# Two transposing DMAs inside SBUF in place of four DMA trips through DRAM in a convolution beside a gated MLP

## The chip, the cores and the metric

The kernel runs on one core of one Trainium2 chip. The metric is device time in microseconds (us), the median over runs of the whole launch. Before the change it is 251.94 us, the median of two runs at 250.64 and 253.25. The profiled execution, from which all durations below come, took 251.85 us. Its span, from the first to the last recorded instruction, is 249.6 us.

## What is computed

The inputs have 2048 positions (S) and 640 channels (D). `A_q` is x, and `xn` is its layer norm over channels. Two branches read `xn` and are added to x:

```
k_shift = four-tap causal convolution of k along S, taps per channel
kv  = k_shift * v
y   = causal convolution of kv with ssm_k along S (by rfft of length 4096) + kv * ssm_D
out = x + xn * y + (sigmoid(xn @ w_gate) * (xn @ w_up)) @ w_down
```

The gated MLP has 1728 hidden columns. All tensors are bf16.

## The kernel before

**The MLP** is the bulk of the matrix work. Positions are cut into four passes of 512. A pass runs 13 gate and up pairs (lines 258 and 270, five matmuls of 512 columns each), a closing pair for the last 64 hidden columns (282), and eight down products (297, 14 matmuls of 320 columns each). ScalarE takes the sigmoid from PSUM (261), VectorE multiplies (276) and adds the down products into x (300). From the second pass on, `xnT` is made by `xn_turn` (233): two DMAs that transpose 128 x 1280 elements each, within SBUF.

**The convolution** goes by five chunks of 128 channels. Each chunk passes these steps:

- `load_k`, `load_v`, `kv_op` (330 to 339): 16 VectorE operations that make kv.
- `h_tr` (315): 16 TensorE transposes of the filter. The weights that they load step by 16 elements, 32 bytes.
- `st1` (357): eight steps of four matmuls; ScalarE copies each step's 128 x 1024 fp32 result from PSUM (360).
- the first turn: four writes `wr1` (366) and four reads `rd2` (375) through a DRAM tile, 512 KB each.
- `st2` (385): four groups of 16 matmuls on 32 x 32 tiles, each followed by two ScalarE copies (388).
- `prod` (397, 399): per group a VectorE shuffle and a product.
- `inv1` (415): for each pair of groups 64 matmuls on 32 x 32 tiles with 256 columns; two ScalarE copies (420) into `ao`.
- the second turn: two writes `wr2` (427) and two reads `rdb` (437) through DRAM, 512 KB each.
- `inv2` (447): four steps of eight matmuls with 128 columns; VectorE multiplies by `xn` (451) and adds into x (452). Then `store` (303) writes out.

**The order** of every engine is fixed when the program is built. A planner in the kernel keeps a free time for every engine, walks along the MLP's steps on TensorE, and puts a step of the convolution between them when its estimated inputs are ready. Engines then run their lists in that order, waiting on semaphores. SyncE (SP, its queue is SPq) issues nearly all DMAs, also in order: a DMA that waits holds up those behind it. The buffers that matter are `psC`, two PSUM tiles for `st1`, `st2` and `inv1`, and the SBUF tiles `kx`, `kvh`, `t`, `xz`, `ao`, `bi`.

Of the kernel before, what the change touches and what calls it, by code (L numbers as in the profile page):

```python
# [19 lines left out]
P = 128  # L20
# [3 lines left out]
NQ = 4  # L24
# [33 lines left out]
def kernel(  # L58
# [31 lines left out]
    dr = ctx.enter_context(tc.tile_pool(name="dr", bufs=1, space=bass.MemoryType.DRAM))  # L90
# [21 lines left out]
    kxs = [res.tile([P, NB + 3, P], BF16, name="kx%d" % i) for i in range(2)]  # L112
    for kx in kxs:
        nc.gpsimd.memset(kx[0:1, 0:3, :], 0.0)
# [37 lines left out]
    def load_k(c, lo, hi):  # L152
        sync.dma_start(kxs[c % 2][:, lo + 3:hi + 3, :], kr[:, lo:hi, c * P:(c + 1) * P])

    def load_halo(c):
        cs = slice(c * P, (c + 1) * P)
        sync.dma_start(kxs[c % 2][16:P, 0:3, :], kr[15:P - 1, NB - 3:NB, cs])
        sync.dma_start(kxs[c % 2][1:16, 0:3, :], kr[0:15, NB - 3:NB, cs])

    def load_v(c, lo, hi):  # L160
        d = cin[c]
        if lo == 0:
            d["kvh"] = cv.tile([P, NB, 2, P], BF16, name="kvh", bufs=2)
        sync.dma_start(d["kvh"][:, lo:hi, 0, :], vr[:, lo:hi, c * P:(c + 1) * P])  # L164
# [17 lines left out]
    def ln_stats(g, i):  # L182
        b = 4 * g + i
        d = lns[g]
        if i == 0:
            d["st"] = cv.tile([P, 4, 2, nc.vector.BN_STATS_DIM], F32, name="st", bufs=2)
            d["mv"] = cv.tile([P, 4, nc.vector.BN_AGGR_DIM], F32, name="mv", bufs=2)
            d["var"] = cv.tile([P, 4], F32, name="var", bufs=2)
            d["rstd"] = cv.tile([P, 4], F32, name="rstd", bufs=2)
            d["nmr"] = cv.tile([P, 4], F32, name="nmr", bufs=2)  # L190
        for s2 in range(2):
            nc.vector.bn_stats(d["st"][:, i, s2, :], x[:, b, s2 * 320:(s2 + 1) * 320])  # L192
        nc.vector.bn_aggr(d["mv"][:, i, :], d["st"][:, i, :, :])
# [124 lines left out]
    def kv_op(c, n):  # L318
# [5 lines left out]
        kx = kxs[c % 2]  # L324
# [21 lines left out]
    def st1(c, n):  # L346

        h, n4 = divmod(n, 4)
        d = chunks[c]
        if n == 0:  # L350
            d["d1"] = dr.tile([P, 2, NB, 2 * P], BF16, name="d1", bufs=2)
        if n % 2 == 0:
            d["t1"] = cv.tile([P, 8, 2, P], BF16, name="t1", bufs=2)
        ps = psC.tile([P, 4, 2 * P], F32, name="ps1", tag="c")
        for i in range(4):
            b = 4 * n4 + i
            nc.tensor.matmul(ps[:, i, :], lhsT=S1[:, b, h, :], rhs=cin[c]["kvh"][:, b, :, :],  # L357
                             start=True, stop=True)
        o = 4 * (n % 2)
        nc.scalar.copy(out=d["t1"][:, o:o + 4, :, :].rearrange("p b s c -> p b (s c)"), in_=ps[:, :, :])  # L360
        d[n // 2] = d["t1"]

    def wr1(c, k):
        h, part = divmod(k, 2)
        d = chunks[c]
        sync.dma_start(d["d1"][:, h, 8 * part:8 * part + 8, :], d[k].rearrange("p b s c -> p b (s c)"))
# [3 lines left out]
    def rd2(s):  # L370

        c, s4 = divmod(s, 4)
        t2 = cv.tile([P, 8, 2 * P], BF16, name="t2", bufs=2)
        src = chunks[c]["d1"].rearrange("(r q) h b e -> r (q h b) e", q=NQ)
        sync.dma_start(t2[:, :, :], src[8 * s4:8 * s4 + 8].rearrange("r p e -> p r e"))
        groups[s] = dict(t2=t2)

    def st2(s):

        d = groups[s]  # L380
        d["xz"] = cv.tile([P, 3, 8, P], BF16, name="xz", bufs=3)
        ps = [psC.tile([P, 2, 2, 2, P], F32, name="ps2", tag="c") for _ in range(2)]
        for g in range(4):
            for q in range(NQ):
                nc.tensor.matmul(ps[q // 2][quad(g), q % 2, :, :, :], lhsT=SM[quad(q), 0, :],  # L385
                                 rhs=d["t2"][quad(q), 2 * g:2 * g + 2, :], start=True, stop=True)
        for n in range(2):
            nc.scalar.copy(out=d["xz"][:, 0:2, 4 * n:4 * n + 4, :].rearrange("p s k c -> p k s c"),  # L388
                           in_=ps[n].rearrange("p q e s c -> p (q e) s c"))
# [3 lines left out]
    def prod(s, n):  # L393

        xz = groups[s]["xz"]
# [6 lines left out]
    def inv1(y):  # L402
# [3 lines left out]
        if y2 == 0:  # L406
            d["d2"] = dr.tile([32, P, P], BF16, name="d2", bufs=2)
        ao = kxs[1][:, 0:NB, :] if y >= 7 and y % 2 else cv.tile([P, 16, P], BF16, name="ao")[:, :, :]
        ps = [psC.tile([P, 2, 512], F32, name="psa", tag="c") for _ in range(2)]
        for o in range(2):  # L410
            xz = groups[2 * y + o]["xz"]
            for i in range(2):
                for q in range(NQ):
                    for g in range(4):
                        nc.tensor.matmul(ps[g // 2][quad(q), g % 2, 256 * o:256 * o + 256], lhsT=SM[quad(g), 1 + i, :],  # L415
                                         rhs=xz[quad(g), 1 + i, 2 * q:2 * q + 2, :],
                                         start=(i == 0), stop=(i == 1))
# [6 lines left out]
    def wr2(y):  # L424
        c, y2 = divmod(y, 2)
        d = chunks[c]
        sync.dma_start(d["d2"][16 * y2:16 * y2 + 16].rearrange("r p c -> p r c"), d["ao", y])

    def rdb(c, n):

        d = chunks[c]
        if c >= 3 and n == 1:
            bi = kxs[0][:, 0:NB, :].rearrange("p (h b) c -> p h b c", h=2)
        else:
            bi = cv.tile([P, 2, 8, P], BF16, name="bi")[:, :, :, :]
        src = d["d2"].rearrange("r (q h b) c -> (r q) h (b c)", q=NQ, h=2)
        sync.dma_start(bi.rearrange("p h b c -> p h (b c)"), src[:, :, 1024 * n:1024 * n + 1024])
        d["bi", n] = bi

    def inv2(c, m):  # L440

        cs = slice(c * P, (c + 1) * P)
        bi = chunks[c]["bi", m // 2]
        ps = psG.tile([P, 4, P], F32, name="psb", tag="g")
        for i in range(4):
            for h in range(2):
                nc.tensor.matmul(ps[:, i, :], lhsT=TB[:, h, 4 * m + i, :], rhs=bi[:, h, 4 * (m % 2) + i, :],  # L447
# [70 lines left out]
    def emit(step):  # L518
# [3 lines left out]
        for eng, dur, need, make in ops:  # L522
            at = when(need)
            if eng == "DMA":
                free["SP"] = max(free["SP"], at) + 0.45
                free["DMA"] = max(free["DMA"], free["SP"] + 1.4) + dur
                end = free["DMA"] + 1.2
            else:
# [21 lines left out]
    def s_st1(c, n):  # L550
        def ops():
            mk, nd = C()
            n4 = n % 4
            k = 4 * c + n // 2
            o = [("PE", 0.45, [nd, "S1", ("kv", c, n4 // 2), ("h", c, n4 // 2)], [("st1", c, n)]),
                 ("ACT", 0.92, [("st1", c, n), prior("d1", k - 2)], [mk, ("t1", c, n)])]
# [3 lines left out]
    def s_wr1(c, i):  # L560
        return s_load(wr1, (c, i), 1.35, [("t1", c, 2 * i + 1)], [("d1", 4 * c + i)])

    def s_rd2(s):
        return rd2, (s,), lambda: [("DMA", 1.8, [("d1", 4 * (s // 4) + i) for i in range(4)]
                                    + [prior("st2", s - 2)], [("t2", s)])]

    def s_st2(s):
        def ops():
# [3 lines left out]
                    ("ACT", 0.92, [("st2", s), prior("inv1", (s - 3) // 2) if s > 2 else None], [m0]),  # L572
# [6 lines left out]
    def aofree(y):  # L579
        if y < 7:  # L580
            return [prior("d2", y - 1)]
        return [("kvn", 3, 15)] if y == 7 else [("d2", y - 2)]

    def s_inv1(y):
        def ops():
            m0, n0 = C()
            m1, n1 = C(1)
            return [("PE", 0.75, [n0, n1, ("prod", 2 * y + 1)], [("inv1", y)]),
                    ("ACT", 0.92, [("inv1", y)] + aofree(y), [m0]),
# [3 lines left out]
    def s_rdb(c, n):  # L593
        if c < 3:
            back = ("inv2", c, 1) if n else prior("inv2", c - 1, 3)
        else:
            back = (("inv2", 2, 3), ("inv2", 3, 1), ("kvn", 4, 15), ("inv2", 3, 3))[2 * n + c - 3]
        return rdb, (c, n), lambda: [("DMA", 1.0, [("d2", 2 * c), ("d2", 2 * c + 1), back], [("bi", c, n)])]

    def s_inv2(c, m):  # L600
        def ops():
            mk, nd = G()
            return [("PE", 0.48, [nd, ("bi", c, m // 2), ("xn", m, 3) if m else None, "TB"], [("inv2", c, m)]),
                    ("DVE", 0.62, [("inv2", c, m)], [mk, ("yx", c, m)]),
                    ("DVE", 0.36, [("yx", c, m)], [("xa", c, m)])]
        return inv2, (c, m), ops

    def s_htr(c, part):
        def ops():
            mk, nd = G()  # L610
            return [("PE", 0.55, [nd, ("D", c), ("va", c)], [("htr", c, part)]),
                    ("ACT", 0.92, [("htr", c, part), prior("st1", c - 2, 7)], [mk, ("h", c, part)])]
# [13 lines left out]
    def s_load(fn, args, occ, need, make):  # L626
        return fn, args, lambda: [("DMA", occ, need, make)]

    chains = dict(sp=[], dve1=[], ln=[], kv=[], pool=[], act=[], inv=[], mid=[], front=[], out=[], sp_b=[], sp_k=[],
                  sp_v=[], sp_t=[], sp_h=[], bulk=[], sp_w1=[], sp_w2=[])  # L630
    for c in range(NC):
        if c:
            last = [prior("kvn", c - 2, 13)]
# [9 lines left out]
            for i in range(4):  # L643
                chains["sp_v"].append(s_load(load_v, (c, 4 * i, 4 * i + 4), 0.7, [prior("st1", c - 2, 7)],
# [6 lines left out]
        chains["sp_w1"] += [s_wr1(c, i) for i in range(4)]  # L651
        for s in range(4 * c, 4 * c + 4):
            chains["sp"].append(s_rd2(s))
            chains["mid"].append(s_st2(s))
            chains["dve1"] += [s_prod(s, 0), s_prod(s, 1)]
            if s % 2:
                chains["inv"].append(s_inv1(s // 2))
                chains["sp_w2"].append(s_load(wr2, (s // 2,), 2.4, [("ao", s // 2)], [("d2", s // 2)]))
        chains["sp_b"] += [s_rdb(c, n) for n in range(2)]
# [36 lines left out]
    def s_turn(g, i):  # L696
        return s_load(xn_turn, (g, i), 1.6, [("pass", g - 1), ("xn", g, i), ("xn", g, i + 1)], [("xT", g, i)])
# [53 lines left out]
    DUE = (8, 48, 52)  # L751
    slack = dict(bulk=3.0, sp_k=3.0, sp_v=3.0, sp_h=1.5, bulk2=1.5)

    def side(now, at):

        again = True
        while again:
            again = False
            for k in ("sp_x", "sp_w1", "sp", "sp_w2", "sp_b", "sp_t", "bulk", "sp_k", "sp_v", "sp_h", "bulk2", "out"):
# [21 lines left out]
    at, credit, TURN, TH = 0, 0, 6, 1.5  # L781
# [58 lines left out]
```

## Time and profile before

| what | value |
|---|---|
| profiled execution | 251.85 us, span 249.6 us |
| TensorE busy | 235.6 us, 94% of the span |
| VectorE busy | 185.1 us, 74% |
| ScalarE busy | 144.4 us, 58% |
| DMA queue q1 | 55.59 MB, 79.8% of 16 DMA engines' span |
| granted TensorE clock | 0.994 |

In the tables of groups a line names the source line, the engine, the operation and its tiles, then the count, the busy time in us and the mean ns of one instruction. PEld is TensorE's weight load, which runs beside its matmuls. The share of a page's chain of waits is the share of the span that the work that ended last spent on an engine. A timeline row has a start, a duration, and in brackets the idle time before it and what ended it. A matmul's duration in a row is longer than the distance to the next one, because matmuls are pipelined; where the path matters, distances between starts are used.

### The profile page before, as it was taken

The page shows a single profiled execution, that of the slowest core. Times are in us where ns is not written, and L with a number is a line of the kernel's source. Part 1 is how long each engine was busy: PE and PEld are TensorE (multiplying, and loading weights), DVE is VectorE, ACT ScalarE, POOL GpSimd, SP SyncE. Part 2 cuts the span into 40 slices and gives each one's busy share as a digit, 9 for nine tenths or more (in the row PEclk, how much of TensorE's full clock was granted, in tenths as well). Part 3 has the DMA queues.
Part 4 walks back from the last instruction along what each step waited for, and adds up shares of the span by engine and source line. Part 5 has one row for each costly group of instructions (what it writes and reads, how often), then busy time and mean ns, then how long its engine had stood idle before and what let it go on. Part 6 is the DMA issues. An engine that isn't in the chain of part 4 may idle for free.

```text
span 249.6 us, 5854 instructions
## 1 busy us (share of the span) xinstructions
PE 235.6 (94%) x2409; PEld 137.5 (55%) x2409; DVE 185.1 (74%) x346; ACT 144.4 (58%) x178; POOL 10.0 (4%) x24
## 2 busy tenths in 40 slices
PE   8799999998999999897999999999999999999970
PEld 2474555776445564565755456456765444466760
DVE  3627997529999999897789999789245865886253
ACT  2652366403888796445698778785665668663000
POOL 4300001000000020020000000000000000000000
PEclk9999999999999999999999999999999999999997
DMA  6998999999998999997589878398787454764544
GB/s 178 286 245 233 332 332 335 286 242 246 221 277 235 330 327 264 232 264 172 231 225 273 253 265 250 90 191 206 217 247 243 115 158 118 223 193 146 132 144 147
DMA packets 96294, 56.81 MB, mean 228 GB/s; under 512 B 56268, under 2 KB 89356, under 8 KB 96012
## 3 DMA queue, kind: packets, MB, share of 16 engines
q1 hardware_dynamic: 95692, 55.59, 79.8%
q10 hardware_dynamic: 576, 0.85, 1.1%
q8 instruction: 19, 0.31, 0.5%
q14 instruction: 7, 0.06, 0.1%
HBM read 36.12 MB, written 18.35 MB: 218 GB/s over the span
## 4 chain that ended last, share of the span: by engine, by line
PE 81%; DMA 7%; DVE 5%; SPq 4%; issue 1%; ACT 1%; DVEq 0%
PE pg L258 22%; PE pu L270 22%; PE pd L297 15%; PE ps L357 7%; DMA bi<-d 3%; PE psa L415 3%; PE psb L447 3%; PE ps L385 3%; DMA t<-d 2%; PE pg L248 2%; PE pg L282 2%; PE pht L315 2%; DMA x<-in_A_q_dram 1%; DVE st L192 1%; DVE yx L451 1%; SPq L164 1%
## 5 line engine op out<-in xcount | busy, mean ns | idle before, releaser
L297 PE MATMUL pd<-wd,hT 128*128 128x320 bf16 x448 | 64.2, 299 | 0.0
L258 PE MATMUL pg<-xnT,w 128*128 128x512 bf16 x250 | 62.2, 380 | 0.0
L270 PE MATMUL pu<-xnT,w 128*128 128x512 bf16 x250 | 62.2, 379 | 0.0
L297 PEld LDWEIGHTS <-hT 128*128 128x128 bf16 x448 | 43.2, 98 | 18.0 <-issue 1.4
L388 ACT CAST xz<-ps 128x1024 bf16<-128x1024 f32 x40 | 38.6, 1018 | 18.8 <-PE ps L385 18.8
L276 DVE TENSOR_TENSOR hT<-sig,pu 128x512 bf16<-128x512 bf16 x49 | 33.4, 681 | 17.2 <-PE pu L270 12.6
L261 ACT ACTIVATE sig<-pg 128x512 bf16<-128x512 f32 x52 | 31.5, 606 | 24.4 <-PE pg L258 21.7
L360 ACT CAST t<-ps 128x1024 bf16<-128x1024 f32 x40 | 38.8, 1016 | 8.7 <-PE ps L357 6.9
L270 PEld LDWEIGHTS <-w 128*128 128x128 bf16 x250 | 23.7, 98 | 27.0 <-issue 1.1
L258 PEld LDWEIGHTS <-w 128*128 128x128 bf16 x250 | 23.3, 98 | 26.7 <-issue 2.0
L300 DVE TENSOR_TENSOR x<-pd,x 128x320 bf16<-128x320 f32 x32 | 15.6, 490 | 24.7 <-PE pd L297 24.6
L399 DVE TENSOR_TENSOR xz<-xz 128x2048 bf16<-128x2048 bf16 x20 | 24.5, 1223 | 0.5
L357 PE MATMUL ps<-kvh,S1t 128*128 128x256 bf16 x160 | 21.6, 273 | 0.0
L336 DVE TENSOR_TENSOR acc<-acc,tmp 128x1024 bf16<-128x1024 bf16 x30 | 20.8, 692 | 1.0
L334 DVE TENSOR_TENSOR tmp<-kx,sc 128x1024 bf16<-128x1024 bf16 x30 | 20.5, 685 | 0.3
L420 ACT CAST ao<-psa 128x1024 bf16<-128x1024 f32 x16 | 15.4, 1015 | 6.7 <-PE psa L415 6.7
L357 PEld LDWEIGHTS <-S1t 128*128 128x128 bf16 x160 | 15.6, 98 | 5.8
L451 DVE TENSOR_TENSOR yx<-psb,xn 128x512 bf16<-128x512 f32 x20 | 13.8, 691 | 4.1 <-PE psb L447 2.8
L316 ACT COPY kvh<-pht 128x1024 bf16<-128x1024 bf16 x10 | 9.7, 1030 | 11.7 <-PE pht L315 11.7
L192 DVE BATCH_NORM_STATS2 st<-x 128x6 f32<-128x320 bf16 x32 | 13.8, 474 | 3.1 <-DMA x<-in_A_q_dram 3.1
L397 DVE STREAM_SHUFFLE xz<-xz 128x512 f32<-128x512 f32 x20 | 14.6, 728 | 0.0
L447 PEld LDWEIGHTS <-TBt 128*128 128x128 bf16 x160 | 9.4, 98 | 3.7 <-issue 1.9
(50 smaller groups left out, 139.9 us busy)
## 6 DMA issues: line engine op xcount, KB each, us to landing
d<-t SPq DMA_DIRECT2D x20, 512.0 KB, 4.2
t<-d SPq DMA_DIRECT2D x20, 512.0 KB, 5.4
d<-ao SPq DMA_DIRECT2D x8, 512.0 KB, 4.5
bi<-d SPq DMA_DIRECT2D x8, 512.0 KB, 5.0
hn<-in_A_ssm_k_dram SPq DMA_DIRECT2D x8, 256.0 KB, 4.5
kx<-in_A_k_dram SPq DMA_DIRECT2D x16, 128.0 KB, 4.8
kvh<-in_A_v_dram SPq DMA_DIRECT2D x16, 128.0 KB, 4.0
x<-in_A_q_dram SPq DMA_DIRECT2D x3, 640.0 KB, 6.2
```

Of the source, the lines that this page charges most:

```text
L258: nc.tensor.matmul(pg[:, :], lhsT=w[:, c, fc * P:(fc + 1) * P], rhs=xnT[:, :, c, :], start=(c == 0), stop=(c == NC - 1))
L261: nc.scalar.activation(sig[fc][:, :], pg[:, :], ACT.Sigmoid)
L270: nc.tensor.matmul(pu[:, :], lhsT=w[:, c, UP + fc * P:UP + (fc + 1) * P], rhs=xnT[:, :, c, :], start=(c == 0), stop=(c == NC - 1))
L276: nc.vector.tensor_tensor(hT[:, fc, :], sig[fc][:, :], pu[:, :], ALU.mult)
L297: nc.tensor.matmul(pd[:, :], lhsT=hT[:, fc, bb * P:(bb + 1) * P], rhs=wd[:, fc, es], start=(fc == 0), stop=(fc == NFC - 1))
L334: nc.vector.tensor_tensor(d["tmp"][:, :, :], kx[:, lo + 3 - m:hi + 3 - m, :], sb(m), ALU.mult)
L336: nc.vector.tensor_tensor(d["acc"][:, :, :], d["acc"][:, :, :], d["tmp"][:, :, :], ALU.add)
L357: nc.tensor.matmul(ps[:, i, :], lhsT=S1[:, b, h, :], rhs=cin[c]["kvh"][:, b, :, :], start=True, stop=True)
L360: nc.scalar.copy(out=d["t1"][:, o:o + 4, :, :].rearrange("p b s c -> p b (s c)"), in_=ps[:, :, :])
L388: nc.scalar.copy(out=d["xz"][:, 0:2, 4 * n:4 * n + 4, :].rearrange("p s k c -> p k s c"), in_=ps[n].rearrange("p q e s c -> p (q e) s c"))
L399: nc.vector.tensor_tensor(xz[:, 1:3, :, :], xz[:, 0:1, :, :].to_broadcast((P, 2, 8, P)), xz[:, 1:3, :, :], ALU.mult)
L447: nc.tensor.matmul(ps[:, i, :], lhsT=TB[:, h, 4 * m + i, :], rhs=bi[:, h, 4 * (m % 2) + i, :], start=(h == 0), stop=(h == 1))
```

## The change

The DRAM tiles and `wr1`, `rd2`, `wr2`, `rdb` go. In their place, `turn1` issues two transposing DMAs for each of the four groups of a chunk (128 x 1024 elements each), and `turn2` issues one for each of its two halves (128 x 2048). For that, ScalarE's copy after `st1` writes its result turned inside the partition: it reads PSUM with a step of 256 fp32 elements and writes runs of four bf16 with a step of 64 bytes. `inv2` reads its moving operand with a step of 32 elements, 64 bytes. Products of two groups share one tile, so `inv1` has half as many matmuls of twice the columns. There is one buffer in place of two or three for `kx`, `kvh`, the products and layer-norm statistics; `t1` now holds a whole chunk once, and `t2` has four buffers.

The planner is given new entries for the turns and new values for two of its constants, so that the order of all engines changes too. In the built program, the last `inv1` of the last chunk has no down product after it, where before it had 84 down matmuls; the last `st2` has 14 down matmuls between it and that `inv1`.

```
-    kxs = [res.tile([P, NB + 3, P], BF16, name="kx%d" % i) for i in range(2)]
+    kx = res.tile([P, NB + 3, P], BF16, name="kx")
...
-            d["kvh"] = cv.tile([P, NB, 2, P], BF16, name="kvh", bufs=2)
+            d["kvh"] = cv.tile([P, NB, 2, P], BF16, name="kvh")
...
-        nc.scalar.copy(out=d["t1"][:, o:o + 4, :, :].rearrange("p b s c -> p b (s c)"), in_=ps[:, :, :])
+            d["t1"] = cv.tile([P, 2 * P, 2, NB], BF16, name="t1")
+        nc.scalar.copy(out=d["t1"][:, :, h, 4 * n4:4 * n4 + 4], in_=ps.rearrange("p b e -> p e b"))
-    def wr1(c, k):
-        sync.dma_start(d["d1"][:, h, 8 * part:8 * part + 8, :], d[k].rearrange("p b s c -> p b (s c)"))
-    def rd2(s):
-        sync.dma_start(t2[:, :, :], src[8 * s4:8 * s4 + 8].rearrange("r p e -> p r e"))
+    def turn1(s):
+        c, s4 = divmod(s, 4)
+        t2 = cv.tile([P, 2, 8, P], BF16, name="t2", bufs=4)
+        for i in range(2):
+            e = P * i + 32 * s4
+            sync.dma_start_transpose(t2[:, i, :, :], chunks[c]["t1"][:, e:e + 32, :, :].rearrange("p e h b -> p (e h b)"))
...
-        d["xz"] = cv.tile([P, 3, 8, P], BF16, name="xz", bufs=3)
+            pairs[y] = cv.tile([P, 3, 2, 8, P], BF16, name="xz")
...
-                        nc.tensor.matmul(ps[g // 2][quad(q), g % 2, 256 * o:256 * o + 256], lhsT=SM[quad(g), 1 + i, :],
-                                         rhs=xz[quad(g), 1 + i, 2 * q:2 * q + 2, :],
+                    nc.tensor.matmul(ps[g // 2][quad(q), g % 2, :], lhsT=SM[quad(g), 1 + i, :],
+                                     rhs=pairs[y][quad(g), 1 + i, :, 2 * q:2 * q + 2, :],
...
-    def wr2(y):
-        sync.dma_start(d["d2"][16 * y2:16 * y2 + 16].rearrange("r p c -> p r c"), d["ao", y])
-    def rdb(c, n):
-        sync.dma_start(bi.rearrange("p h b c -> p h (b c)"), src[:, :, 1024 * n:1024 * n + 1024])
+    def turn2(y):
+            d["bi"] = cv.tile([P, P, 2, NB], BF16, name="bi")
+        sync.dma_start_transpose(d["bi"][:, 64 * y2:64 * y2 + 64, :, :].rearrange("p (g a) h b -> p g (a h b)", a=4),
+                                 d["ao", y].rearrange("p r c -> p (r c)"))
...
-                nc.tensor.matmul(ps[:, i, :], lhsT=TB[:, h, 4 * m + i, :], rhs=bi[:, h, 4 * (m % 2) + i, :],
+                nc.tensor.matmul(ps[:, i, :], lhsT=TB[:, h, 4 * m + i, :], rhs=bi[:, :, h, 4 * m + i],
...
-    DUE = (8, 48, 52)
+    DUE = (8, 56, 80)
...
-    at, credit, TURN, TH = 0, 0, 6, 1.5
+    at, credit, TURN, TH = 0, 0, 1, 1.5
```

## The prediction

> **What bounds the kernel now.** I read the page's busy table, slices and chain first.
>
> ```profile
> PE 235.6 (94%) x2409; PEld 137.5 (55%) x2409; DVE 185.1 (74%) x346; ACT 144.4 (58%) x178; POOL 10.0 (4%) x24
> ...
> PE   8799999998999999897999999999999999999970
> ...
> PE 81%; DMA 7%; DVE 5%; SPq 4%; issue 1%; ACT 1%; DVEq 0%
> ```
>
> TensorE is busy 235.6 of 249.6 us; the 14.0 us without it lie in the first slice and the last two. A step taken from another engine or a DMA wins nothing unless TensorE was waiting for it. So I read the table of waits for TensorE and its weight loads:
>
> ```profile
> PEld L385 <- DMA t<-d: 2.3, 2, 1.3
> ...
> PE ps L385 <- DMA t<-d: 1.7, 2, 0.9
> PE psb L447 <- DMA bi<-d: 1.6, 1, 1.6
> ```
>
> The columns are total us, times, longest. Weight loads and matmuls wait side by side, so the trips through DRAM cost TensorE 1.7 + 1.6 = 3.3 us: that is all the change can win in mid-stream. The rest is the tail, from the timeline:
>
> ```profile
> 225.41 0.73 DVE L397 STREAM_SHUFFLE xz<-xz 128x512 f32<-128x512 f32 x1
> ...
> 226.18 1.23 DVE L399 TENSOR_TENSOR xz<-xz 128x2048 bf16<-128x2048 bf16 x1
> ...
> 227.76 0.84 PE L415 MATMUL psa<-xz,SMt 32*32 32x256 bf16 x64
> ...
> 228.53 11.58 PE L297 MATMUL pd<-wd,hT 128*128 128x320 bf16 x84
> 228.62 1.93 ACT L420 CAST kx<-psa 128x1024 bf16<-128x1024 f32 x2 [3.97 <-PE psa L415]
> 230.57 0.37 SPq L427 DMA_DIRECT2D d<-kx  x1
> ...
> 239.95 1.06 PE L447 MATMUL psb<-bi,TBt 128*128 128x128 bf16 x16
> ```
>
> The last inv1 ends at 228.60. Its copies, write and read then run beside 84 down matmuls, and the first inv2 of the last chunk starts at 239.95, when these end. From there to the end of the span are 9.69 us: four VectorE steps of about 1.25 us (the products start at 240.60, 241.85, 243.11, 244.36), then the stores.
>
> **The tail after the change.** TensorE's work is the same but for two terms below. The new order has all 84 down matmuls ahead of the last inv1, so that step can start at 227.76 + (239.95 - 228.53 = 11.42) = 239.18, if the stream before it loses as much as now. What it waits for is later still. Only 14 down matmuls, 14 x (11.42 / 84 = 0.136) = 1.9 us, stand between the last st2 and it, while its input needs two copies (1.93, the pair at 228.62; st2's have the same shape), a shuffle (0.73), a product (1.23) and about 0.3 of handing over (0.02 to 0.2 at each hand in these rows): 4.2 us. TensorE waits 2.3.
>
> Behind inv1 nothing is left to hide anything. Two copies take it from 228.60 to 230.57 today, 1.97 us with the issue. Then comes the new turn. Its nearest row is the transposing DMA that the kernel has already, ten blocks of 128 x 128 within SBUF; one line's view has its time on SP's queue (least, median, most ns) and its landing from issue:
>
> ```profile
> L233 SPq DMA_TRANSPOSE xnT<-xn x6: 1342/1856/4044, 47.2 to 167.4; - x6
> ...
> DMA to landing us min/median/max: 3.5/4.4/6.2
> ```
>
> The last turn has 16 blocks, and the DMA engines are idle then. Bounds: 3.5 (ten blocks' least) and 6.2 x 1.6 = 9.9. I take the low side, 3.5 + 6 x 0.134 (1.342 / 10) = 4.3, with 0.4 for handing over: 4.7. Sum: 239.18 + 2.3 + 0.84 (inv1) + 1.97 + 4.7 + 9.69 = 258.7, against 249.64: **+9.0 us**.
>
> **TensorE's own terms.** inv2's moving operand now steps by 64 bytes. No matmul here streams with such a step; the nearest rows are weight loads, one with a step of 32 bytes and one without:
>
> ```profile
> L447 PEld LDWEIGHTS <-TBt 128*128 128x128 bf16 x160 | 9.4, 98 | 3.7 <-issue 1.9 <-DMA bi<-d 0.9
> ...
> L315 PEld LDWEIGHTS <-hn 128*128 128x128 bf16 x80 | 5.7, 148 | 0.1
> ```
>
> 128 stepped columns take 50 ns more. Weight loads hide beside matmuls, so sixteen h_tr steps take 1.00 us on the chain against 0.89 for sixteen inv2 matmuls: 7 ns more each. A moving operand has no such cover. Bounds: 0 and, no row excluding worse than the load's, twice 50 ns; I take 50. Four chunks of 32 matmuls: 128 x 50 = 6.4 us; in the last chunk only the first step's eight count (0.4), the others hide under VectorE's 1.25 us. **+6.8 us.**
>
> [...]
>
> inv1's 32 matmuls of 512 columns replace 64 of 256, the same columns. By st2 (16 of 512 in 0.44 us on the chain) they take 0.88, against 0.77 now; equal columns say no change. I take half of 0.11, ten times: **+0.5 us**.
>
> **What I cost at nothing.** *ScalarE's copy after st1* (40 of them, 1.016 us now) gets a stepped PSUM read; no row has one. Bounds: 1.0 and 2.0. The nearest is the taps' copy with an 8-byte step in SBUF (128x512, 0.664 us) beside the 128x512 sigmoid (0.606): 0.11 ns per element more, 1.13 us by that. ScalarE has 105 us free, and 4 us more over the kernel lie beside TensorE's work.
>
> *The first turn.* From the last st1 of a chunk to its first st2 the new order has 7 to 12 us of TensorE work. The need: a copy and its handing over (1.2), the first DMA on SP for eight blocks (1.1 to 1.8), the landing of the second (3.5 to 6.2): 5.8 to 9.2. The 3.3 us of waits today may go, or such waits replace them. I take neither.
>
> *SP and DMA traffic.* Fifty transposing DMAs cost SP between 0.134 and 0.228 us per block (1.342, and 13.65 us for the six over 60): 480 blocks, 64 to 109 us. The 60 removed issues were 0.33 to 0.53 each, 24 us. SP has room in sum. The 60 removed transfers were 31 MB of 56.8, the new turns are 15 MB read and written once.
>
> *Single buffers.* kvh's next v load waits for st1's last step, kx's for the chunk's last tap, the pair tile's copies for the inv1 before: all lie under 2 us or more of MLP work in the new order. VectorE's operations keep their count and sizes.
>
> **Sum.** 249.6 + 9.0 + 6.8 + 0.5 = 265.9 of span; the execution is 2.2 longer than its span (251.85 - 249.6), and 0.1 from the median shown. **268 us**, 6.4% slower.
>
> **Rivals.**
>
> *The step costs inv2 nothing*, or the 7 ns of h_tr: 268 - 6 = **262**. For it: the weight loads' excess is latency. Against: nothing hides a moving operand. 0.22.
>
> *The stepped PSUM read is slow*: ScalarE's copy at 2.0 us. st1's steps alternate two PSUM tiles, and a chunk's last five or six stand within 5 to 8 us of TensorE work. The last must wait for the copy of the second before it, four copies after the second step of the run: 4 us at 1.0, just covered, 8 at 2.0, so 3 to 4 us of TensorE lost in four chunks and about 1 in the spread-out last, 15 in all: **283**. Against: the taps' copy. 0.16.
> [...]
>
> *SP is held.* Chunk 1's v load stands on SP behind eight turn DMAs and two xn turns, and VectorE's list needs it about 20 us after them. At the median rate it lands about in time; at 4.0 us for ten blocks the eight take 25 us, and VectorE, hence the PSUM tiles of up, stands 4 to 12 us. Taken at 8: **276**. For: the six DMAs spread threefold. 0.12.
>
> *Not slower*: the trips through DRAM are what holds the present stream. Along the order, TensorE's distances add up to 5.3 us less than its clock shows from the first h_tr to the last down product, 3.3 of it the waits above. If short turns clear all of it, steps cost nothing and the last turn lands in 3.5, 249.6 - 5.3 + 8.2 + 2.2 = **255**, within 2%. To be faster, the tail too would have to be covered; the order leaves it only 1.9 us. 0.08.
>
> My forecast has 0.42. The range takes in the rivals from 257 (the second case, less 3.3 for waits that go and 1 for the landing) to 282. Left out are the last rival and half of the slow copies, 0.16. A measurement here tells about 2%, 5 us, from no change: faster (below 246.9) 0.03, within 0.08, slower (above 257.0) 0.89.
>
> **What would show it.** Behind the last down matmul, about 16 us of span with a last inv1, a DMA and then inv2; a last turn landing in 4 to 5 us; 16 inv2 matmuls in 1.6 to 1.8 us instead of 0.89; st1's copies near 1.1 us; TensorE's waits for turns in mid-stream no longer than 4 us. A first inv2 of the last chunk hidden under down products, or busy TensorE time falling, would prove me wrong.

## The result and the profile after

The changed kernel takes 282.27 us (median of 282.16 and 282.39) against 251.94: 1.120 times as long, 95% interval 1.095 to 1.145. The direction was right; the size was not. 268 was forecast, and 282.3 lies just beyond the end of the range at 282. The span of the profiled execution is 280.5 us, 30.9 more than before.

The page of the changed kernel: busy time by engine, the slices of TensorE and of its granted clock, and the chain.

```profile
PE 262.9 (94%) x2089; PEld 144.8 (52%) x2089; DVE 186.3 (66%) x346; ACT 144.3 (51%) x177; POOL 10.1 (4%) x23
...
PE   7899999999999999999999999999999999997072
...
PEclk9999999999999999999999999995999995999655
...
PE 3%; DMA 2%; issue 1%; DVE 0%; ACT 0%; ACTq 0%
```

VectorE and ScalarE have the busy time that they had (186.3 us against 185.1, 144.3 against 144.4). TensorE is busy 27.3 us longer, with 320 instructions fewer, so some of them became dearer. Two slices of the clock in mid-stream read 5, half speed. The same line of the kernel before has none:

```profile
PEclk9999999999999999999999999999999999999997
```

The chain could be followed back for 7% of the span only, which is no use here.

The groups by line and shape, of the changed kernel (count, then busy us and mean ns), name the dear ones:

```profile
L354 ACT CAST t<-ps 128x1024 bf16<-128x1024 f32 x40 | 39.1, 1016 | 11.4 <-PE ps L352 11.1
...
L429 PE MATMUL psb<-bi,TBt 128*128 128x128 bf16 x160 | 36.2, 393 | 6.4 <-DMA bi<-ao 6.4
...
L405 PE MATMUL psa<-xz,SMt 32*32 32x512 bf16 x320 | 6.5, 379 | 2.9 <-DVE xz L393 2.9
```

inv2's 160 matmuls are busy 36.2 us; before they were busy 8.6 + 2.1. ScalarE's copy with the stepped PSUM read is at 1016 ns exactly what the plain one was. The distance between inv2's matmuls is read from TensorE's timeline of the changed kernel, here at full clock in mid-stream:

```profile
82.60 3.62 PE L429 MATMUL psb<-bi,TBt 128*128 128x128 bf16 x16
86.05 1.05 PE L352 MATMUL ps<-kvh,S1t 128*128 128x256 bf16 x8
```

Sixteen take 86.05 - 82.60 = 3.45 us; the median distance from one to the next is 0.217. In the kernel before, sixteen start at 239.95 and the next sixteen here:

```profile
240.84 1.06 PE L447 MATMUL psb<-kx,TBt 128*128 128x128 bf16 x16
```

That is 0.89 us, 0.056 each. The moving operand with a step of 64 bytes costs TensorE four times the time, 0.161 us more per matmul.

The clock, in windows of the changed kernel around the second dip (us; busy time of TensorE and its weight loads, VectorE, ScalarE, GpSimd; granted clock; DMA share; GB/s):

```profile
234.00:235.00 1.00, 1.00 (x5) 0.49 (x4) 0.41 (x2) 0.00 (x0) 0.00 (x0) 0.50 0.97 181
...
238.00:239.00 1.00, 1.00 (x21) 0.28 (x19) 0.45 (x1) 0.10 (x1) 0.00 (x0) 1.00 1.04 307
```

and TensorE's timeline just there:

```profile
227.71 7.11 PE L429 MATMUL psb<-bi,TBt 128*128 128x128 bf16 x32
234.65 2.31 PE L256 MATMUL pg<-xnT,w 128*128 128x512 bf16 x5
236.75 1.69 PE L268 MATMUL pu<-xnT,w 128*128 128x512 bf16 x5
238.38 0.43 PE L378 MATMUL ps<-t,SMt 32*32 32x512 bf16 x16
```

Thirty-two stepped matmuls run for 6.9 us, and behind them five gate matmuls take 2.10 us and five up matmuls 1.63, where 1.08 is usual. The same happens at 193.49, behind the other run of 32, to seven down and five gate matmuls. Together 1.02 + 0.54 + 0.89 + 0.67 = 3.1 us. The record of the granted clock agrees. It reads 0.5 from 189.86 to 196.69 and from 230.82 to 237.65, that is from 3.1 to 3.3 us after the start of each run to 3.0 to 3.2 us behind its end; half of these 6.2 us behind the runs is 3.1. The stepped matmuls keep their 0.217 us at either clock: 32 of them have a row of 7.11 us here, and one of 7.11 at 267.90, where the clock is at 0.5 all along.

The tail of the changed kernel, from its timeline:

```profile
255.87 2.08 PE L295 MATMUL pd<-wd,hT 128*128 128x320 bf16 x14
...
260.85 0.66 PE L405 MATMUL psa<-xz,SMt 32*32 32x512 bf16 x32 [2.90 <-DVE xz L393]
261.64 1.93 ACT L410 CAST ao<-psa 128x1024 bf16<-128x1024 f32 x2 [2.86 <-issue]
267.90 6.63 PEld L429 LDWEIGHTS <-TBt 128*128 128x128 bf16 x32 [6.84 <-DMA bi<-ao]
267.90 7.11 PE L429 MATMUL psb<-bi,TBt 128*128 128x128 bf16 x32 [6.39 <-DMA bi<-ao]
```

inv1 stands behind the last down product, waits 2.9 us for its product, and inv2 waits 6.4 us for copies and turn. The new turns' own rows, from one line's view each (ns on SP's queue, then us from issue to landing; first the 16 blocks of `turn2`, then the eight of `turn1`):

```profile
L419 SPq DMA_TRANSPOSE bi<-ao x10: 1829/2010/6008, 63.5 to 263.6; - x10
...
DMA to landing us min/median/max: 4.3/4.5/9.3
```

```profile
L366 SPq DMA_TRANSPOSE t<-t x40: 1232/1339/2181, 44.3 to 235.7; - x40
...
DMA to landing us min/median/max: 3.2/3.4/5.1
```

### The profile page after: what moved, and what is told of

It is laid out like the page before. It is cut to its first block, busy times and chain, and to the rows that moved or that the text cites. A ratio compares the mean times of both kernels' runs of the same rounds, so it can differ in the third digit from the quotient of the medians.

```text
span 280.5 us, 5208 instructions
## 1 busy us (share of the span) xinstructions
PE 262.9 (94%) x2089; PEld 144.8 (52%) x2089; DVE 186.3 (66%) x346; ACT 144.3 (51%) x177; POOL 10.1 (4%) x23
## 5 line engine op out<-in xcount | busy, mean ns | idle before, releaser
L295 PE MATMUL pd<-wd,hT 128*128 128x320 bf16 x448 | 66.0, 302 | 0.5 <-DVE hT L284 0.5
L256 PE MATMUL pg<-xnT,w 128*128 128x512 bf16 x250 | 63.9, 387 | 0.0
L274 DVE TENSOR_TENSOR hT<-sig,pu 128x512 bf16<-128x512 bf16 x50 | 34.1, 682 | 28.6 <-PE pu L268 23.0
L381 ACT CAST xz<-ps 128x1024 bf16<-128x1024 f32 x40 | 38.5, 1016 | 22.6 <-PE ps L378 11.9
L354 ACT CAST t<-ps 128x1024 bf16<-128x1024 f32 x40 | 39.1, 1016 | 11.4 <-PE ps L352 11.1
L429 PE MATMUL psb<-bi,TBt 128*128 128x128 bf16 x160 | 36.2, 393 | 6.4 <-DMA bi<-ao 6.4
L256 PEld LDWEIGHTS <-w 128*128 128x128 bf16 x250 | 24.5, 100 | 27.6 <-issue 2.9
L268 PEld LDWEIGHTS <-w 128*128 128x128 bf16 x250 | 24.1, 99 | 28.0 <-issue 3.2
L429 PEld LDWEIGHTS <-TBt 128*128 128x128 bf16 x160 | 18.2, 116 | 22.7 <-DMA bi<-ao 6.8
L410 ACT CAST ao<-psa 128x1024 bf16<-128x1024 f32 x20 | 19.3, 1018 | 18.4 <-PE psa L405 15.4
L433 DVE TENSOR_TENSOR yx<-psb,xn 128x512 bf16<-128x512 f32 x20 | 13.8, 692 | 20.8 <-PE psb L429 20.5
L331 DVE TENSOR_TENSOR tmp<-kx,sc 128x1024 bf16<-128x1024 bf16 x30 | 20.6, 685 | 0.2
```

What stands on the lines that cost most here:

```text
L256: nc.tensor.matmul(pg[:, :], lhsT=w[:, c, fc * P:(fc + 1) * P], rhs=xnT[:, :, c, :], start=(c == 0), stop=(c == NC - 1))
L268: nc.tensor.matmul(pu[:, :], lhsT=w[:, c, UP + fc * P:UP + (fc + 1) * P], rhs=xnT[:, :, c, :], start=(c == 0), stop=(c == NC - 1))
L274: nc.vector.tensor_tensor(hT[:, fc, :], sig[fc][:, :], pu[:, :], ALU.mult)
L295: nc.tensor.matmul(pd[:, :], lhsT=hT[:, fc, bb * P:(bb + 1) * P], rhs=wd[:, fc, es], start=(fc == 0), stop=(fc == NFC - 1))
L331: nc.vector.tensor_tensor(d["tmp"][:, :, :], kx[:, lo + 3 - m:hi + 3 - m, :], sb(m), ALU.mult)
L354: nc.scalar.copy(out=d["t1"][:, :, h, 4 * n4:4 * n4 + 4], in_=ps.rearrange("p b e -> p e b"))
```

## The experiments

### The step taken away

```
-                nc.tensor.matmul(ps[:, i, :], lhsT=TB[:, h, 4 * m + i, :], rhs=bi[:, :, h, 4 * m + i],
+                flat = bi.rearrange("p c h b -> p (c h b)")
+                nc.tensor.matmul(ps[:, i, :], lhsT=TB[:, h, 4 * m + i, :], rhs=flat[:, h * 2048 + 128 * (4 * m + i):h * 2048 + 128 * (4 * m + i) + 128],
```

> The changed kernel, with the same order and waits, but inv2 reads 128 adjacent elements of bi for each matmul instead of 128 elements at a step of 64 bytes (so it multiplies other elements than the convolution needs). Theory A (the step of the moving operand is nearly all of the loss): the distance between inv2's matmuls falls from 0.217 us to 0.056, 128 of them in mid-stream give back 20.6 us, the clock stays at 1.0 in mid-stream, which gives back another 2 to 3 us, and from the first inv2 of the last chunk to the end of the span it takes 9.7 us, not 12.6: a span of 253 to 256, a time of 255 to 258. Rival B (inv2's matmuls are slow because bi is written by transposing DMAs, or because other engines use SBUF at that time): the distance stays above 0.15 us and the time above 270.

Measured: 256.87 us, 1.020 times the kernel before (1.012 to 1.027); span 255.6. The order is that of the changed kernel, instruction by instruction, and the DMAs write bi as they did. The run of 32 that took 6.9 us takes 213.26 - 211.48 = 1.78 here, 0.056 each, and the clock stays at 1.0 in mid-stream:

```profile
PEclk9999999999999999999999999999999999999555
```

```profile
211.48 1.95 PE L430 MATMUL psb<-bi,TBt 128*128 128x128 bf16 x32
213.26 1.24 PE L256 MATMUL pg<-xnT,w 128*128 128x512 bf16 x5
```

So 25.4 of the 30.3 us of loss go with the step. They are 128 x 0.161 = 20.6 in the first four chunks, 3.1 of clock, and the longer tail: the last inv2 to the end takes 255.6 - 245.45 = 10.15 us here and 280.5 - 267.90 = 12.6 there. These sum to 26.1, against a difference of spans of 24.9. That TensorE is slow because of DMA writes or its neighbours is refuted.

What is left, 5 to 6 us over before, is a dearer tail less what a shorter stream gives back. TensorE's waits in this run show the tail:

```profile
PE psb L430 <- DMA bi<-ao: 6.2, 1, 6.2
PE psa L405 <- DVE xz L393: 2.9, 1, 2.9
```

The last inv1 starts at 237.98, though it waited 2.9; with before's stream it would start at 239.18 without that wait. So the new stream runs 239.2 + 2.9 - 238.0 = 4.1 us shorter than the old. The three waits for DRAM trips are gone (0.93, 0.74 and 1.56 us of idle TensorE, 3.2 in all), and nine inv1 are 0.19 us shorter each (1.7). A new wait of 0.5 for VectorE's `hT` and one of 0.3 for its `yx` stand against them, which makes 4.1.

### Other steps

```
+        step = (16, 8, 4, 2, 1)[c]
...
+                at = h * 2048 + (4 * m + i) % step
-                nc.tensor.matmul(ps[:, i, :], lhsT=TB[:, h, 4 * m + i, :], rhs=bi[:, :, h, 4 * m + i],
+                nc.tensor.matmul(ps[:, i, :], lhsT=TB[:, h, 4 * m + i, :], rhs=flat[:, at:at + 127 * step + 1:step],
```

> The changed kernel, but inv2's moving operand has another step in each chunk: 16, 8, 4, 2 and 1 elements (32, 16, 8, 4 and 2 bytes) for chunks 0 to 4 (so it multiplies other elements than the convolution needs). Read from the distances between inv2's matmuls. [...] Rival A2 (the price grows with the step): 0.056 at 2 bytes, about 0.06, 0.11 and 0.2 at 4, 8 and 16. Rival A3 (any step costs the same): 0.217 from 4 bytes on.

The whole took 271.56 us in its one run, which says little with five steps in it. Measured (median distance of one chunk's matmuls; the two ends from the kernels named):

| step, bytes | 2 | 4 | 8 | 16 | 32 | 64 |
|---|---|---|---|---|---|---|
| us per 128-column matmul | 0.056 (before) | 0.057 | 0.116 | 0.228 | 0.232 | 0.217 (after) |

Three rows of TensorE's timeline of this run, for steps of 32, 8 and 4 bytes:

```profile
83.22 3.88 PE L432 MATMUL psb<-bi,TBt 128*128 128x128 bf16 x16
...
189.51 3.89 PE L432 MATMUL psb<-bi,TBt 128*128 128x128 bf16 x32
...
225.90 1.98 PE L432 MATMUL psb<-bi,TBt 128*128 128x128 bf16 x32
```

Sixteen matmuls at 32 bytes last as long as 32 at 8 bytes, and 32 at 4 bytes half of that. A step of 4 bytes costs what 2 bytes do (0.057 us against 0.056), 8 bytes twice as much (0.116), 16 bytes and more four times (0.217 to 0.232), and no more beyond. Neither A2 nor A3 is right as a whole. A2's numbers (0.06, 0.11, 0.2) are near up to 16 bytes, but the price stops growing there. A3 fails at 4. In numbers of this table one column costs 0.056 / 128 = 0.44 ns at 2 bytes, 0.91 at 8 and 1.7 to 1.8 from 16 on. Where the first column starts was not varied by itself.

### The step put into the kernel before

```
-                nc.tensor.matmul(ps[:, i, :], lhsT=TB[:, h, 4 * m + i, :], rhs=bi[:, h, 4 * (m % 2) + i, :],
+                at = 8 * h + 4 * (m % 2) + i
+                nc.tensor.matmul(ps[:, i, :], lhsT=TB[:, h, 4 * m + i, :], rhs=flat[:, at:at + 127 * 16 + 1:16],
```

> The kernel before, with one edit: inv2's moving operand steps by 16 elements, 32 bytes, through bi (so it multiplies other elements than the convolution needs). If the step alone makes the loss, and 32 bytes cost what 64 do, 128 matmuls of the first four chunks cost 20.6 us more, the tail 2 to 3 more, and the clock falls behind long runs of such matmuls (1 to 3 us): 276 to 279. If half that per matmul: 263 to 266. If the loss needs the transposing DMAs: 252.

Measured: 284.74 us, 1.131 times before (1.120 to 1.141), with inv2's distance at 0.233. With no turn, buffer or order changed, the step costs 33 us. The distances give 128 x 0.177 = 22.7, and from the last chunk's first inv2 to the end it takes 282.5 - 269.57 = 12.9 us in place of 9.7. The gate, up, down and st1 matmuls take 7.0 us more between starts than in the kernel before. That is the clock: before the last chunk's inv2 it is at 0.5 for 17.1 us (of 27.1 in the span, by the mean of 0.952), 3.3 of them under stepped matmuls, and half of the other 13.8 is 6.9. Its slices on the page of this run, 7.06 us each:

```profile
PEclk9999999999999999989999999999977999869975
```

One of these places in the timeline:

```profile
199.85 3.89 PE L449 MATMUL psb<-bi,TBt 128*128 128x128 bf16 x16
203.67 0.95 PE L415 MATMUL psa<-xz,SMt 32*32 32x256 bf16 x64
204.55 2.31 PE L270 MATMUL pu<-xnT,w 128*128 128x512 bf16 x5
206.66 1.75 PE L258 MATMUL pg<-xnT,w 128*128 128x512 bf16 x5
```

This is more than the 276 to 279 expected, since 32 bytes cost a little more than 64 (0.233 us against 0.217) and the clock cost 6.9 us where 1 to 3 were expected.

### Stepped runs broken up

```
+            if k == "last" and before == "last" and at < len(seq):
+                continue
...
+            before = pick
```

`before` holds the kind of step that was placed last, and "last" is the kind of inv2's steps.

> The changed kernel with its stepped reads, but no inv2 step stands directly behind another in the order while MLP steps are left (the four of a chunk stood together for chunks 2 and 3). Theory C (a run of about 7 us of stepped matmuls makes the clock fall to one half behind it; the profile shows 3.1 us lost so, 0.89 + 0.67 at 193.5 to 197.1 and 1.02 + 0.54 at 234.7 to 238.4): the clock stays at 1.0 up to the tail and 3 us are given back, if the new order's tail costs the same; the order has both last st2 steps together, which costs 2 more: 281 to 282, with the granted clock above 0.955 over the span. Rival (the clock follows the average over a longer time, or something else): slices below 0.9 in mid-stream remain.

Measured: 284.07 us (1.127; 1.124 to 1.130) where 281 to 282 was expected; span 281.2, clock 0.960. The clock stayed up in mid-stream, as theory C has it, in the page of this run:

```profile
PEclk9999999999999999999999999999999999999555
```

No slice in mid-stream is below 0.9. With runs of eight stepped matmuls, 1.7 us, and other work between them, the clock is 1.00 in each stretch of 10 us from 180 to 250; with runs of 32 in the changed kernel it fell. The time didn't fall: in the new order the last st2 steps stand together without cover and wait 1.7 us for copies, and the last inv1 waits 4.4.

It isn't the length of a run alone. What the matmuls behind a run took, by the distances between starts in TensorE's timelines (elsewhere in mid-stream eight st1 matmuls take 0.87 to 0.88 us, seven down matmuls 0.96, five gate or up matmuls 1.08):

| run | step, bytes | matmuls, us | behind them, us |
|---|---|---|---|
| after, 82.60 | 64 | 16, 3.45 | eight st1 0.89 |
| steps, 83.22 | 32 | 16, 3.69 | eight st1 1.69, five gate 1.81 |
| steps, 189.51 | 8 | 32, 3.72 | seven down 0.96, five gate 1.08 |
| before_step, 199.85 | 32 | 16, 3.82 | behind inv1 five up 2.11, five gate 1.59 |
| after, 186.56 | 64 | 32, 6.93 | seven down 1.84, five gate 1.75 |
| after, 227.71 | 64 | 32, 6.94 | five gate 2.10, five up 1.63 |

Of three runs of sixteen two are followed by slow matmuls and one is not, and 3.72 us at 8 bytes are not either. What decides it was not shown: no run was made to test this, and other work near the run may count too.

### The tail alone, in the kernel before

```
+            if k == "inv" and pos["inv"] == 9 and at < len(seq):
+                continue
```

> The kernel before, with the last inv1 held back in the order until all down products are placed, so that its copies, its two DMA trips and the last inv2 have nothing beside them. The tail theory: inv1 starts near 239.2 in the span, ends 0.8 later, copies take 2.0, write and read through DRAM 9 (230.57 to 239.8 at most today, with a read landing 5.0 us after its issue at 234.43), then 9.7 to the end: a span of 260 to 261, a time of 262 to 263.5. Rival (the uncovered tail is given back, since the stream before it runs shorter): 252 to 255.

Measured: 262.17 us, 1.041 (1.031 to 1.051). The timeline of this run:

```profile
239.26 0.84 PE L415 MATMUL psa<-xz,SMt 32*32 32x256 bf16 x64
...
240.12 1.93 ACT L420 CAST kx<-psa 128x1024 bf16<-128x1024 f32 x2 [15.38 <-PE psa L415]
...
250.08 1.89 PE L447 MATMUL psb<-bi,TBt 128*128 128x128 bf16 x16 [9.98 <-DMA bi<-d]
```

inv1 starts at 239.26, where 239.18 was worked out, and the trip stands bare. A last inv1 without cover costs 10.6 us (260.2 - 249.6 of span) when the turn goes through DRAM.

### The pair tile alone, in the kernel before

```
-        d["xz"] = cv.tile([P, 3, 8, P], BF16, name="xz", bufs=3)
+            pairs[y] = cv.tile([P, 3, 2, 8, P], BF16, name="xz")
...
-                            nc.tensor.matmul(ps[g // 2][quad(q), g % 2, 256 * o:256 * o + 256], lhsT=SM[quad(g), 1 + i, :],
+                    nc.tensor.matmul(ps[g // 2][quad(q), g % 2, :], lhsT=SM[quad(g), 1 + i, :],
...
-                    ("ACT", 0.92, [("st2", s), prior("inv1", (s - 3) // 2) if s > 2 else None], [m0]),
+                    ("ACT", 0.92, [("st2", s), prior("inv1", s // 2 - 1)], [m0]),
```

> The kernel before, DRAM trips and dense reads kept, with the pair tile of the change alone: one buffer for the products of two groups, inv1 as 32 matmuls of 512 columns. The planner, told of the single buffer, now puts the last inv1 behind all down products by itself. Theory T (the single pair buffer is what moves the end of the chain behind the down products): inv1 takes 0.59 us instead of 0.77 (1.8 us less in ten), and the tail costs what it did when inv1 was held back (10.6 us): 259 to 262. Rival (the tail comes from the single kvh and kx or from the turns): 249 to 253.

Measured: 262.64 us, 1.041 (1.038 to 1.044), 0.6 above the end of what was expected. This one edit, in the old kernel, is enough to move the last inv1 behind all down products: with one pair tile the planner lets a group's copies wait for the inv1 before them. The tail follows:

```profile
239.57 0.65 PE L416 MATMUL psa<-xz,SMt 32*32 32x512 bf16 x32 [0.84 <-DVE xz L402]
...
250.35 1.87 PE L448 MATMUL psb<-bi,TBt 128*128 128x128 bf16 x16 [10.12 <-DMA bi<-d]
```

This run and the dense one both end uncovered; they differ in turns (and the buffers and order that go with them), and the dense one is 5.8 us faster: from the end of the last copy to inv2 its bare turn takes 245.45 - 241.13 = 4.3 us, against 250.35 - 242.24 = 8.1 through DRAM, and mid-stream waits for DRAM go. Whether the pair tile alone, or also the single t1 and kvh, move the tail in the changed kernel wasn't separated.

### A copy that makes the read dense

One more step per half chunk copies bi into a tile with adjacent channels; t2 has two buffers instead of four for the room. ScalarE copies in one kernel, GpSimd in the other.

```
+        for h in range(2):
+            nc.scalar.copy(out=d["bd"][:, h, :, cs], in_=d["bi"][:, cs, h, :].rearrange("p c b -> p b c"))
...
-                nc.tensor.matmul(ps[:, i, :], lhsT=TB[:, h, 4 * m + i, :], rhs=bi[:, :, h, 4 * m + i],
+                nc.tensor.matmul(ps[:, i, :], lhsT=TB[:, h, 4 * m + i, :], rhs=bd[:, h, 4 * m + i, :],
```

> The changed kernel with one more step: ScalarE copies bi, as each half lands, into a tile in which the 128 channels of one position are adjacent, and inv2 reads that (t2 has two buffers instead of four for the room). inv2's distance 0.056 us and the clock at 1.0 in mid-stream as in the dense run (256.9), plus two copies of 1.0 us behind the last turn, plus 2 to 3 since the new order has both last st2 steps together: 259 to 264. If ScalarE pays for its 64-byte step as TensorE does (0.22 us per 128 elements, 1.8 us per copy of 1024), 262 to 268.

> The same with GpSimd making that copy (it is idle but for 4% of the span). By its copy of the taps (128x512 in 0.638 us) 1.3 us per 1024 elements: 260 to 264. [...] Rival: its reads of SBUF hold up VectorE, and the time is above 268.

Measured: 279.90 us with ScalarE, 273.75 with GpSimd (1.110 with 1.106 to 1.114, and 1.085 with 1.079 to 1.092). Both are better than the change and far from the kernel before. The copies' rows, first ScalarE's, then GpSimd's, from the view of bi in each run:

```profile
L430 ACT COPY bd<-bi x20: 1899/1932/1988, 75.3 to 266.4; 128x1024 bf16<-128x1024 bf16 x20
```

```profile
L430 POOL COPY bd<-bi x20: 1886/1918/2933, 71.8 to 260.5; 128x1024 bf16<-128x1024 bf16 x20
```

A copy costs ScalarE 1.93 us, where its copies of the same size out of PSUM cost 1.02, stepped or not. Whether it pays for the step in SBUF was not shown, as no plain copy of this size out of SBUF was run. ScalarE's copy is near the dearer of the prices expected for it (1.8), GpSimd's, at 1.92, above the 1.3 expected. The copies don't explain the times by themselves: TensorE waits 14.0 and 12.2 us for them, 8.8 and 8.5 of that in one wait each, and the order is another. With GpSimd VectorE's product takes 1.415 us on the mean instead of 1.223, and VectorE's busy time grows by 8.9 us; the rival that it is held up and the time lies above 268 fits in sign, but what this costs TensorE was not separated. Both expectations counted the copy and not the waits around it, and missed.

## Why the prediction was wrong

**The step of the moving operand** is the term that failed. The prediction took 50 ns per 128 columns from the weight loads' excess, with "twice 50 ns" as the upper bound, although it said that nothing hides a moving operand. It costs 161 ns, above that bound: 20.6 us in mid-stream in place of 6.4, and 2.5 us more in the tail, where TensorE (1.7 us per step) and no longer VectorE (1.25) sets the pace. That the step costs TensorE time was right; its size was not. No rival had it dearer. The weight loads' 50 ns were too low by a factor of three.

**The clock** was no term at all: 3.1 us, behind the two runs of 32 stepped matmuls.

**The tail** was right in its mechanism: inv1 with no work behind it. The wait before inv1 was 2.9 (2.3 forecast), the turn 4.3 with the handing over (4.7), its landing 4.26. In the dense run, which has no step, the time is 5 us over before and not 9, because of the next two.

**The waits of mid-stream** were put at no gain. They went, 3.2 us (0.93, 0.74 and 1.56 of idle TensorE), and one of 0.5 for VectorE came. The first turn's cover of 7 to 12 us held, with landings of 3.4 us. The prediction's first reading of the page missed these waits: of the 14.0 us without TensorE, 3.0 lie in the first two slices, 7.7 in the last two and 3.2 in mid-stream. Its table of waits then had them.

**inv1** was put at +0.5, by st2's matmuls. It fell from 0.77 to 0.58, 1.9 us in ten: the wrong sign. Half of the excess of another shape, the st2 row, was no estimate.

Added to the forecast span of 265.9, to the last inv1: 20.6 - 6.4 for the step, 3.1 for the clock, 0.6 for the longer wait, less 2.7 of waits (3.2 - 0.5) and 2.2 of inv1's sign (0.5 + 1.7); then 2.5 in the tail less 0.4 of the turn, come to 281.0, against 280.5 measured. 0.5 us are not accounted for.

**What was costed at nothing** held: the stepped PSUM read (1016 ns before and after), SP (1.34 us on the median per `turn1`, 2.01 per `turn2`), VectorE. The rival of slow copies gave 283, close to the result, for a reason that the profile refutes, so its number is luck: its 2.0 us per copy was the author's bound, and the runs showed 1.016. The end of the range at 282 leans on this rival, and that the range nearly holds the result is luck as well. SP was not held: TensorE's only wait in mid-stream is the 0.5 us named above. The rival that the change is not slower had the stream right in part: without the step, clearing it gave 4.1 of the 5.3 us it named, but the tail cost more than that.

No version tried beats the kernel before. Dense reads together with the new turns come to 1.020 of it, and the time that they lack is that of a covered tail; as run, they multiply other elements than the convolution needs.

## What to carry to other kernels

Ask of every changed access pattern how TensorE will stream it. In the table of steps, 128 bf16 columns out of SBUF take 0.056 to 0.057 us up to a step of 4 bytes, twice that at 8 (0.116) and four times from 16 on (0.217 to 0.232); other widths and types were not run. A layout that saves a transfer can cost more on the engine that is the bound than the transfer ever did: here 20.6 us in mid-stream, against 3.2 of waits for the trips. And when a buffer is merged or halved, look at the order for what now stands last: a chain that ends behind the last cover pays its full latency once, however short its steps are (10.6 us in the kernel before with its last inv1 held back).

## What the runs showed of the hardware

- TensorE's moving operand in bf16, per 128 columns: 0.056 us at a step of 2 bytes, 0.057 at 4, 0.116 at 8, 0.228 at 16, 0.232 at 32, 0.217 at 64. With the granted clock at 0.5 in the tail the 64-byte step still takes 0.217, while dense matmuls there (dense run) go from 0.056 to 0.107: the halved clock made the dense ones slower and not the stepped ones.
- In the changed kernel the granted clock drops to 0.5 in mid-stream 3.1 to 3.3 us after the start of each run of 32 such matmuls (6.9 us) and comes back 3.0 to 3.2 us behind its end, though TensorE is busy throughout (7.00 of 7.00 us from 227 to 234). In spread, with runs of eight (1.7 us) and other work between them, it is 1.00 from 180 to 250. What decides between the two was not shown.
- ScalarE's copy of 128 x 1024 out of PSUM takes 1016 ns with a step of 1 KB as without one, and it takes 1932 ns for 128 x 1024 out of SBUF at a step of 64 bytes; a plain copy of that size out of SBUF was not run.
- A transposing DMA within SBUF lands 3.4 us after its issue for eight 128 x 128 blocks and 4.5 for sixteen (medians), where a write and a read through DRAM took 8.1 us bare in the pair run.
- inv1 as 32 matmuls of 512 columns on 32 x 32 tiles takes 0.58 us, as 64 of 256 columns 0.77.
